# Batch 2's gate and value layer in seven products in place of eight, its weight sums made in batch 1, and the passage to layer two by halves in batches 2 and 3

## The chip, the cores and the metric

One core of one Trainium2 chip runs the whole program. The metric is the device time of one execution in microseconds (us), the median of several runs. A difference under about 0.3% (3.1 us here) can't be told from none.

## What is computed

Linear attention on 4 batches of 8 heads, 576 positions, then two feed-forward layers on the 2304 tokens, all in fp32:

```python
proj = q @ w_phi                      # and k @ w_phi; 64 -> 128 features
proj = proj - max(abs(proj), -1)      # phi = [exp(proj), exp(-proj)]
x = (phi_q @ (phi_k.T @ v)) / (phi_q @ sum(phi_k) + 1e-6)   # tokens x 512
x = leaky_relu(x @ w_in) @ w_out                            # layer one, d_ff 2048
g = x @ w_gate                                              # layer two, d_ff 1536
out = (g * sigmoid(g) * (x @ w_val)) @ w_out2
```

## The kernel before, in words

Work goes batch by batch. The activations of a batch lie with features on the 128 partitions and the 576 tokens (`S`) along the row; a product is made for half of the tokens at a time (`HT` = 288 columns), so that a result fits one PSUM bank. To reach fp32 accuracy every operand is split into a high and a low part of type fp32r: ScalarE copies the high part (`cp`, L90), VectorE subtracts it from the value for the low part (`sub`, L78). A product of two such operands is three matmuls: high by high, high by low, low by high.

A layer-one or gate or value tile of 128 output features takes 4 (the 512 inputs) x 3 = 12 matmuls a half, 24 a tile (`u_l1` L840, `u_gate` L848, `u_val` L859, all through `products` L811). An output block of layer one or two (`u_out` L873) takes four tiles' results at a time, 12 matmuls a half, and is added up in `acc` over the chunks of four.

Where a layer is done "in seven", two such tiles (rows 0 and 1 of weights) by two halves of tokens make a 2 x 2 block product, which `Quad` (L956) computes with seven block products instead of eight: `p1` to `p7`, six matmuls each (`six`, L929). For this it needs sums of the blocks of x (`x_sums_f32` L905) and of the weights (`mix` L788). `Quad` leaves partial results in PSUM bank `a` (p1, then p6, p5 and p3 on top) and bank `e` (p7, then p4 on top). ScalarE copies `a` out after p1, p6 and p5 (`u1`, `u2`, `u4`) before the next product may go on top of it, and VectorE adds them (`add` L990).

Before the change, batch 3 is in seven in both layers (`seven` L1091), batch 2 in layer one only (`seven_beside` L1154); batches 0, 1 and layer two of batch 2 are in eight. While batch b is in its two feed-forward layers, the attention of batch b + 1 runs beside it: its steps for k in layer one, those for q in layer two (`spread`, L1251), evenly over the list of units. A unit is one call of the list `units`; the weights of a unit are loaded and split when the unit four places before it is reached (`slots`, L1217). Each step is written down in the order of the program, and a scheduler then sets the order on each engine.

Weights: the fp64 inputs are turned into fp32 in batch 0 on ScalarE and VectorE (`f32_steps`), kept in HBM (`kept`), split in batch 1 (`w_split` L756), and from then on loaded as parts. The sums for `gX`, `gY`, `vX`, `vY` that batch 3's layer two needs were made beside batch 2's layer two (`w_sums` L797, called at L1292): two loads, four VectorE operations of 256 columns and two stores for each of 12 pairs of tiles. Buffers in SBUF: `wi` has 8 of 4 KB a partition for raw weights and split gate, value and layer-one tiles; `wo` has 5, `wr` 4.

```python
two(x.p1, x.p2, w=[("1", b, 4 * m)])                     # seven_beside, L1179
if not last or halves[-1] == 0:                          # u_out, L887: the parts of x2
    return                                               # are made once both halves are there
```

## Time and profile before

| | |
|---|---|
| median of 3 runs | 1045.04 us (1044.15 to 1047.02) |
| the profiled execution's own time | 1046.1 us |
| its span, first to last instruction | 1044.3 us |
| TensorE (PE) matmul busy | 1035.1 us, 99%, 7638 matmuls |
| weight loads (PEld) busy | 1017.0 us, 97% |
| VectorE (DVE) busy | 791.9 us, 76% |
| ScalarE (ACT) busy | 648.1 us, 62% |
| granted TensorE clock | 1.00 throughout |

Matmuls are pipelined, so the busy time of PE says little of how dense they are; the number of matmuls in a stretch against its length says more. The stages stand in the trace so: opening to 57 us; batch 0 to about 317; batch 1 to 574 (its layer two from about 437); batch 2's layer one to 690, its layer two from 704 to 834; batch 3's layer one to 933, its layer two to the end.

### The profile page before, as it was taken

How to read it: one execution, taken by the hardware profiler on the slowest of the kernel's cores; microseconds unless marked ns; L12 is line 12 of the kernel's file. 1: busy time of each engine (PE TensorE's matmuls, PEld its weight loads, DVE VectorE, ACT ScalarE, POOL GpSimd, SP SyncE). 2: the span in 40 equal slices, each digit the busy share in tenths (PEclk: the TensorE clock that was granted, in tenths of full speed). 3: DMA queues.
4: the chain of work that ended last, by engine and by line, in shares of the span. 5: the costliest groups of instructions: out<-in, count | busy, mean ns of one | idle time of the engine just before them, and what ended most of it. 6: DMA issues, size and time to landing. Idle time of an engine off the chain costs nothing.

```text
span 1044.3 us, 20425 instructions
## 1 busy us (share of the span) xinstructions
PE 1035.1 (99%) x7638; PEld 1017.0 (97%) x7638; DVE 791.9 (76%) x1726; ACT 648.1 (62%) x1448; POOL 21.7 (2%) x57
## 2 busy tenths in 40 slices
PE   9999999999999999999999999999999999999998
PEld 8889999999999999999999999999999999999998
DVE  5988989799999989678776867768788532468463
ACT  6879988699976887456542667735453244436531
POOL 1001100000000000000000000000000000000000
PEclk9999999999999999999999999999999999999999
DMA  8239878367757987856534487266988496559531
GB/s 261 98 145 326 288 272 300 116 221 225 257 198 272 392 320 254 327 195 217 175 130 154 164 308 236 72 245 250 324 287 283 151 321 239 168 186 314 187 112 56
DMA packets 101491, 236.19 MB, mean 226 GB/s; under 512 B 19856, under 2 KB 35984, under 8 KB 101392
## 3 DMA queue, kind: packets, MB, share of 16 engines
q1 hardware_dynamic: 95888, 219.74, 60.7%
q0 software_dynamic: 4032, 14.68, 3.7%
q8 instruction: 61, 1.00, 0.4%
q10 hardware_dynamic: 1472, 0.46, 0.2%
q14 instruction: 38, 0.31, 0.1%
HBM read 169.30 MB, written 65.54 MB: 225 GB/s over the span
## 4 chain that ended last, share of the span: by engine, by line
PE 90%; ACT 4%; DVE 3%; DMA 2%; issue 1%; SPq 0%; ACTq 0%
PE pm L816 61%; PE pa L945 9%; PE pm L945 6%; PE pa L459 5%; PE pa L248 2%; PE pa L207 2%; PE pa L260 2%; DMA xl<-in_vt_dram 1%; ACT wr L691 1%; ACT wi L694 1%; DMA wi<-in_w_dram 1%; PE pa L367 1%; PE pa L366 1%; PE pa L420 1%; DVE xl L78 1%
## 5 line engine op out<-in xcount | busy, mean ns | idle before, releaser
L816 PE MATMUL pm<-xh,wi 128*128 128x288 f32 x1664 | 349.8, 297 | 0.2 <-ACT es L844 0.2
L816 PE MATMUL pm<-gp,wo 128*128 128x288 f32 x2172 | 328.8, 297 | 0.4 <-DVE acc L886 0.2
L816 PEld LDWEIGHTS pm<-gp,wo 128*128 128x128 f32 x2172 | 301.1, 188 | 1.9 <-ACT acc L90 0.5
L816 PEld LDWEIGHTS pm<-xh,wi 128*128 128x128 f32 x1664 | 271.2, 188 | 1.5 <-ACT es L844 0.5
L816 PE MATMUL pm<-xl,wi 128*128 128x288 f32 x832 | 246.2, 297 | 0.0
L816 PEld LDWEIGHTS pm<-xl,wi 128*128 128x128 f32 x832 | 156.2, 188 | 0.6
L886 DVE TENSOR_TENSOR acc<-pm,acc 128x288 f32<-128x288 f32 x160 | 70.6, 451 | 47.8 <-PE pm L816 47.1
L78 DVE TENSOR_TENSOR gp<-es,gp 128x576 fp32r<-128x576 f32 x94 | 70.6, 752 | 26.2 <-ACT gp L90 25.8
L90 ACT ACTIVATE gp<-es 128x576 fp32r<-128x576 f32 x94 | 65.3, 697 | 31.8 <-DVE es L864 26.9
L78 DVE TENSOR_TENSOR wi<-wr,wi 128x512 fp32r<-128x512 f32 x96 | 64.5, 683 | 9.0 <-ACT wi L737 8.0
L737 ACT ACTIVATE wi<-wr 128x512 fp32r<-128x512 f32 x92 | 58.1, 650 | 13.6 <-PE pm L816 5.5
L945 PE MATMUL pm<-xh,wi 128*128 128x288 f32 x272 | 62.0, 296 | 0.1
L78 DVE TENSOR_TENSOR fl<-ff,fh 128x512 fp32r<-128x512 f32 (+1 forms) x72 | 51.2, 714 | 11.8 <-ACT fh L90 11.5
L691 ACT ACTIVATE wr<-wi 128x512 f32<-128x512 f32 x68 | 47.5, 699 | 10.5 <-DVE wi L78 4.2
L719 DVE TENSOR_TENSOR wr<-wr,wi 128x512 uint16<-128x512 uint16 x68 | 50.9, 755 | 0.6
L465 ACT ACTIVATE dn<-pa 64x288 f32<-64x288 f32 x64 | 26.0, 406 | 36.4 <-PE pa L459 35.5
L90 ACT ACTIVATE fh<-ff 128x512 fp32r<-128x512 f32 (+1 forms) x72 | 47.4, 663 | 0.7
L694 ACT ACTIVATE wi<-wi 128x512 int32<-128x512 uint32 x68 | 47.7, 702 | 0.0
L945 PEld LDWEIGHTS pm<-xh,wi 128*128 128x128 f32 x272 | 46.2, 188 | 0.6 <-ACT xh L90 0.3
L844 ACT ACTIVATE es<-pm 128x288 f32<-128x288 f32 x72 | 31.2, 439 | 23.7 <-PE pm L945 14.7
L90 ACT ACTIVATE acc<-pm 128x288 f32<-128x288 f32 x64 | 27.9, 447 | 27.0 <-PE pm L816 26.9
L864 DVE SCALAR_TENSOR_TENSOR es<-pm,es 128x288 f32<-128x288 f32 x72 | 32.1, 448 | 15.4 <-PE pm L816 15.1
(222 smaller groups left out, 2096.9 us busy)
## 6 DMA issues: line engine op xcount, KB each, us to landing
wo<-parts SPq DMA_DIRECT2D x77, 512.0 KB, 5.0
wi<-parts SPq DMA_DIRECT2D x68, 512.0 KB, 5.6
parts<-wi SPq DMA_DIRECT2D x56, 512.0 KB, 5.7
wi<-in_w_dram SPq DMA_DIRECT2D x44, 512.0 KB, 5.2
wr<-kept SPq DMA_DIRECT2D x64, 256.0 KB, 5.1
parts<-wo POOLq DMA_DIRECT2D x28, 512.0 KB, 5.5
kept<-wr SPq DMA_DIRECT2D x40, 256.0 KB, 4.4
wi<-in_wg_dram SPq DMA_DIRECT2D x12, 512.0 KB, 5.6
```

Of the source, the lines that this page charges most:

```text
L78: keep(dve.tensor_tensor(out=o, in0=a, in1=b, op=ALU.subtract))
L90: keep(act.activation(o, a, AF.Copy))
L459: keep(pe.matmul(ps, w, x, start=(i == 0), stop=(i == len(ops) - 1)))
L691: after_opening(act.activation(t[0], high.bitcast(F32), AF.Abs, scale=REBIAS))
L694: after_opening(act.activation(low, low.bitcast(U32), AF.Copy, scale=2.0**-29))
L719: keep(dve.tensor_tensor(out=t16, in0=t16, in1=e16, op=ALU.add))
L737: i = act.activation(t[:, 0], r, AF.Copy)
L816: m = pe.matmul(ps, w, x[:, c], start=(i == 0), stop=(i == n - 1))
L844: act.activation(o, i, AF.Prelu, alpha=0.01)
L864: dve.scalar_tensor_tensor(out=g[:, c], in0=ps, scalar=0.5, in1=g[:, c], op0=ALU.mult, op1=ALU.mult)
L886: dve.tensor_tensor(out=acc[o][:, t], in0=ps, in1=acc[o][:, t], op=ALU.add)
L945: m = pe.matmul(ps, a, b, start=start and n == 0, stop=stop and n == 5, skip_group_check=True)
```

## The change

- Layer two of batch 2 is done by a new `second_beside` with `Quad` for gate and value: seven products for each pair of tiles. The list of its units starts with the last output blocks of layer one, then come six pairs of gate and value tiles; a pair with no output blocks in the queue (the first two, the fourth and the sixth) is 7 units of 12 matmuls, one with them (third and fifth) 11 units.
- The sums of gate and value weights are made in batch 1, in `w_split`, from the fp32 tiles that are there for the split anyway, and stored. `w_sums` with its 24 loads is gone. In batch 2 the sums are loaded and split into two parts (24 tiles of 512 columns); in batch 3 they are loaded as before.
- Passage to layer two in batches 2 and 3: the output blocks come in the order `BY_HALF`, first halves first; the parts of x2 are made by halves (`x2_half`), and only the three quarters that the seven products read; the sums of x2 are made in place in `acc` (`x_sums_in_place`), first those for p7 and p5, then the others. The first pair of batch 3's layer two starts with p1, p2 of gate and value, then both p7, and then p6, p6, p5.
- Buffers: `wi` 8 becomes 5, with 3 new ones of the same size (`wx`) for every second raw weight of batch 0 and for sums of x2 in batch 2; `wr` 4 becomes 5; gate and value tiles of batch 2 take `wo`. Weights are loaded at most 5 ahead in batches 2 and 3 (`depth`), 8 before.

```diff
+BY_HALF = ((0, 0), (1, 0), (2, 0), (3, 0), (0, 1), (2, 1), (1, 1), (3, 1))
...
-        tag = ("wi", 8)
-        if key[0] in "23":
+        tag = ("wi", 5)
+        if key[0] in "gv" and key[1] == QA:
+            tag = ("wo", 5)
...
@@ w_split
+        if len(kind) == 2 and b == QA:
+            wtile[key] = t = T([P, 2, 512], F32R, "wi", 5)
+            to_wtile(t, r)
+            return
...
+        if f % 2 == 0:
+            wf["even", kind] = r
+            return
+        even = wf.pop(("even", kind))
+        mix(even, r)
+        for name, x in (("X", even), ("Y", r)):
...
+                kept[kind + name, f // 2] = d = dram.tile([P, 512], F32, name=f"sums_{uid[0]}")
+                nc.sync.dma_start(out=d, in_=x)
...
+    def x2_half(b, o, t):
+        c = slice(HT * t, HT * t + HT)
+        if o < 2:
+            if t:
+                return
+            if o == 0:
+                x2h[b, "low"], x2l[b, "low"] = T([P, S], F32R, "xh", 8), T([P, S], F32R, "xl", 8)
+            to, h, l = slice(HT * o, HT * o + HT), x2h[b, "low"], x2l[b, "low"]
+        else:
+            if t == 0:
+                x2h[b, o], x2l[b, o] = T([P, S], F32R, "xh", 8), T([P, S], F32R, "xl", 8)
+            to, h, l = c, x2h[b, o], x2l[b, o]
+        cp(h[:, to], acc[o][:, c])
+        sub(l[:, to], acc[o][:, c], h[:, to].bitcast(F32))
...
+    def x_sums_in_place(b):
+        one, two = slice(0, HT), slice(HT, S)
+        rows = [[whole_x.pop((b, kt)) for kt in (k, k + 2)] for k in range(2)]
+        for x in rows:
+            sub(x[0][:, one], x[0][:, two], x[0][:, one])
+            sub(x[0][:, two], x[1][:, two], x[0][:, two])
+        for k, x in enumerate(rows):
+            sums_to_parts(0, k, x[0], b == QA)
+        for x in rows:
+            sub(x[1][:, two], x[1][:, two], x[0][:, one])
+            sub(x[1][:, one], x[1][:, one], x[1][:, two])
+        for k, x in enumerate(rows):
+            sums_to_parts(1, k, x[1], b == QA and k == 0)
...
+    def second_beside(b):
...
+            if not queue:
+                two(*([lambda: x_sums_in_place(b)] if p == 0 else []), x.p1, x.p2, w=[("g", b, 2 * p)])
+                two(y.p1, y.p2, w=[("v", b, 2 * p)])
+                two(x.p7, y.p7, w=[(gy, b, p), (vy, b, p)])
+                two(x.p6, y.p6, w=[(gx, b, p), (vx, b, p)])
+                two(x.p5, y.p5)
+                two(x.p3, y.p3)
+                two(x.p4, y.p4, w=[("g", b, 2 * p + 1), ("v", b, 2 * p + 1)])
...
-        return 4 if any(k[1] == 1 for k in nxt) else 8
+        if any(k[1] == 1 for k in nxt):
+            return 4
+        return 8 if nxt and nxt[0][1] == 0 else 5
```

How the instructions stand, at three places. The first is VectorE at the passage from layer one to layer two of batch 2, from the last output blocks of layer one (`acc`) on; `fl`, `pk`, `mm`, `mrow`, `top` belong to the attention of batch 3. Before:

```order
L78 TENSOR_TENSOR xl_9623<-acc_8645,xh_9622 128x576
L397 CAST mm_78<-top_9744 18x32
L886 TENSOR_TENSOR acc_8678<-pm_9654,acc_8678 128x288
L78 TENSOR_TENSOR pk_10581<-raw_10529,pk_10581 64x576
L78 TENSOR_TENSOR mm_78<-top_9744,mm_78 18x32
L78 TENSOR_TENSOR xl_9669<-acc_8678,xh_9668 128x576
L406 TENSOR_TENSOR mrow_9592<-mm_78,cst_sb 128x288
L78 TENSOR_TENSOR fl_9679<-ff_9675,fh_9678 128x576
L78 TENSOR_TENSOR fl_9740<-ff_9736,fh_9739 128x576
```

With the change:

```order
L894 TENSOR_TENSOR acc_8768<-pm_9744,acc_8768 128x288
L396 TENSOR_REDUCE top_9891<-pa_9842 18x32
L80 TENSOR_TENSOR acc_8735<-acc_8735,acc_8616 128x288
L80 TENSOR_TENSOR wx_9774<-acc_8616,wx_9774 128x576
L80 TENSOR_TENSOR wi_9939<-wr_9768,wi_9939 128x512
L1042 TENSOR_TENSOR vraw_9798<-pm_9800,vraw_9798 128x288
L80 TENSOR_TENSOR acc_8684<-acc_8768,acc_8684 128x288
L399 CAST mm_78<-top_9891 18x32
L80 TENSOR_TENSOR xl_9678<-acc_8768,xh_9677 128x288
L80 TENSOR_TENSOR acc_8735<-acc_8735 128x288
L1042 TENSOR_TENSOR xg_9819<-pm_9821,xg_9819 128x288
L80 TENSOR_TENSOR fl_9835<-ff_9831,fh_9834 128x576
```

Before, the last add of layer one is followed by the last low part of x2 (L78 `xl<-acc`) and by attention, then by the gate's L857. Now sums of x2 (`acc<-acc`), a low part of a sum (`wx`), a split of a weight sum (`wi<-wr`) and the gate's and value's adds (L1042) stand between them.

The second is TensorE in the same layer. Before, the first gate tile follows the last output block with its 24 matmuls in two banks:

```order
L816 MATMUL pm_9654<-mrow_9326,wo_9231 128x288
L816 MATMUL pm_9654<-pk_9327,wo_9231 128x288
L816 MATMUL pm_9654<-mrow_9326,wo_9231 128x288
L816 MATMUL pm_9654<-gp_9464,wo_9231 128x288 x3
L816 MATMUL pm_9654<-gp_9500,wo_9231 128x288 x3
L816 MATMUL pm_9691<-xh_9533,wi_9288 128x288
L816 MATMUL pm_9691<-xl_9534,wi_9288 128x288
```

With the change, at the end of y.p2 and the start of the two p7:

```order
L994 MATMUL pm_9821<-xh_9677,wo_9493 128x288
L994 MATMUL pm_9821<-xl_9678,wo_9493 128x288
L994 MATMUL pm_9821<-xh_9677,wo_9493 128x288
L994 MATMUL pm_9846<-wx_9774,wi_9713 128x288 x3
L461 MATMUL pa_9979<-fh_9834,kvh_8523 128x288
L368 MATMUL pa_10002<-pk_9996,wst_h 128x288
L369 MATMUL pa_10002<-pk_9996,wst_l 128x288
L994 MATMUL pm_9853<-wx_9774,wi_9718 128x288 x3
L994 MATMUL pm_9846<-wx_9777,wi_9713 128x288
L994 MATMUL pm_9853<-wx_9777,wi_9718 128x288
```

The two p7 read the sums of x2 in `wx`, whose low parts VectorE makes after the last add above, 24 matmuls of p1 and p2 and two of attention after the last output block.

The third is VectorE at the passage of batch 3. Before, from the last add of layer one:

```order
L886 TENSOR_TENSOR acc_11904<-pm_12601,acc_11904 128x288
L78 TENSOR_TENSOR acc_11857<-acc_11904,acc_11857 128x288
L78 TENSOR_TENSOR xl_12616<-acc_11904,xh_12615 128x576
L78 TENSOR_TENSOR xl_12640<-acc_11750,xh_12639 128x576
L78 TENSOR_TENSOR acc_11904<-acc_11904,acc_11857 128x288
L78 TENSOR_TENSOR xl_12644<-acc_11813,xh_12643 128x576
L78 TENSOR_TENSOR acc_11904<-acc_11904 128x288
```

With the change:

```order
L894 TENSOR_TENSOR acc_12015<-pm_12718,acc_12015 128x288
L80 TENSOR_TENSOR acc_11970<-acc_12015,acc_11970 128x288
L1042 TENSOR_TENSOR rb_12792<-pm_12783,dn_12781 128x288
L80 TENSOR_TENSOR xl_12653<-acc_12015,xh_12652 128x288
L80 TENSOR_TENSOR acc_12015<-acc_12015,acc_11970 128x288
L80 TENSOR_TENSOR xl_12759<-acc_11970,xh_12758 128x576
L80 TENSOR_TENSOR acc_12015<-acc_12015 128x288
L80 TENSOR_TENSOR xl_12767<-acc_11926,xh_12766 128x576
```

Before, six low parts of 576 columns (`xl`) followed the last add, two of x2's own and four of sums. Now a low part of 288 columns (`xl_12653`) and three of sums follow it.

## Rows read from the trace of the kernel before

**Rows 1.** The page, busy time of each engine over the span.

```profile
PE 1035.1 (99%) x7638; PEld 1017.0 (97%) x7638; DVE 791.9 (76%) x1726; ACT 648.1 (62%) x1448; POOL 21.7 (2%) x57
```

**Rows 2.** Stretches: length; PE, PEld, DVE, ACT, POOL busy (count); clock; DMA; GB/s.

```profile
57.00:182.00 125.00, 123.63 (x917) 120.93 (x917) 112.36 (x234) 109.78 (x260) 10.74 (x23) 1.00 0.74 264
182.00:304.00 122.00, 121.46 (x860) 117.39 (x858) 112.35 (x242) 105.33 (x218) 4.25 (x8) 1.00 0.61 201
...
439.00:574.00 135.00, 135.00 (x1023) 135.00 (x1022) 98.48 (x218) 65.24 (x142) 0.00 (x0) 1.00 0.51 174
574.00:690.00 116.00, 115.32 (x878) 114.33 (x877) 82.54 (x169) 74.10 (x161) 0.00 (x0) 1.00 0.56 194
...
704.00:737.00 33.00, 33.00 (x251) 33.00 (x250) 29.33 (x73) 17.80 (x40) 0.00 (x0) 1.00 0.72 258
737.00:778.00 41.00, 41.00 (x312) 41.00 (x311) 30.24 (x79) 18.56 (x44) 0.00 (x0) 1.00 0.90 315
778.00:802.00 24.00, 24.00 (x183) 24.00 (x182) 21.09 (x55) 10.65 (x25) 0.00 (x0) 1.00 0.83 291
802.00:834.00 32.00, 32.00 (x244) 32.00 (x243) 21.14 (x46) 8.80 (x17) 0.00 (x0) 1.00 0.46 157
...
915.00:942.00 27.00, 26.14 (x191) 25.23 (x190) 18.15 (x39) 9.31 (x18) 0.00 (x0) 1.00 0.60 204
```

**Rows 3.** Chain of waits: start, us, piece (a run of 72 matmuls).

```profile
677.81 9.51 PE pm L816 x72
```

**Rows 4.** VectorE, timeline in batch 2's layer two: start, duration, instruction.

```profile
779.32 0.75 DVE L78 TENSOR_TENSOR gp<-es,gp 128x576 fp32r<-128x576 f32 x1
779.99 0.45 DVE L857 SCALAR_TENSOR_TENSOR es<-es,pm 128x288 f32<-128x288 f32 x1
780.36 0.45 DVE L78 TENSOR_TENSOR xl<-xf,xh 128x288 fp32r<-128x288 f32 x1
...
781.76 0.48 DVE L370 TRANSPOSE_TENSOR_REDUCE cst_sb<-pa 128x9 f32<-128x288 f32 x1
782.16 0.42 DVE L864 SCALAR_TENSOR_TENSOR es<-pm,es 128x288 f32<-128x288 f32 x1
782.51 0.74 DVE L78 TENSOR_TENSOR fl<-ff,fh 128x576 fp32r<-128x576 f32 x1
783.16 0.45 DVE L864 SCALAR_TENSOR_TENSOR es<-pm,es 128x288 f32<-128x288 f32 x1
```

**Rows 5.** VectorE groups in batch 1's layer two: busy, mean ns.

```profile
L78 DVE TENSOR_TENSOR wi<-wr,wi 128x512 fp32r<-128x512 f32 x17 | 11.7, 685 | 2.5 <-ACT wi L737 2.2
```

**Rows 6.** VectorE groups in batch 2's layer two (weight sums, gate and value).

```profile
L864 DVE SCALAR_TENSOR_TENSOR es<-pm,es 128x288 f32<-128x288 f32 x24 | 10.6, 446 | 4.4 <-PE pm L816 4.3
L857 DVE SCALAR_TENSOR_TENSOR es<-es,pm 128x288 f32<-128x288 f32 x24 | 10.6, 444 | 2.0 <-ACT es L856 1.8
L78 DVE TENSOR_TENSOR wr<-wr,wr 128x256 f32<-128x256 f32 x24 | 9.8, 407 | 0.1
...
L792 DVE TENSOR_TENSOR wr<-wr 128x256 f32<-128x256 f32 x12 | 5.1, 423 | 10.6 <-DMA wr<-kept 10.5
L78 DVE TENSOR_TENSOR wr<-wr 128x256 f32<-128x256 f32 x12 | 4.8, 403 | 0.1
```

**Rows 7.** TensorE, timeline at the passage of batch 3: start, duration, instruction.

```profile
934.01 0.29 PE L945 MATMUL pa<-xh,wi 128*128 128x288 f32 x1
934.38 0.40 PE L945 MATMUL pm<-xh,wi 128*128 128x288 f32 x1
934.95 0.40 PE L945 MATMUL pa<-xh,kvl 128*128 128x288 f32 x1 [0.17 <-ACT xh L90]
...
938.90 0.29 PE L945 MATMUL pa<-xh,kvl 128*128 128x288 f32 x1
939.31 0.40 PE L945 MATMUL pa<-xl,kvh 128*128 128x288 f32 x1
939.55 0.29 PE L945 MATMUL pa<-xh,kvh 128*128 128x288 f32 x1
940.34 0.40 PE L945 MATMUL pa<-xh,kvl 128*128 128x288 f32 x1 [0.50 <-ACT raw L90]
940.58 0.30 PE L945 MATMUL pa<-xl,kvl 128*128 128x288 f32 x1
```

**Rows 8.** The page, DMA issues: KB each, median us to landing.

```profile
wo<-parts SPq DMA_DIRECT2D x77, 512.0 KB, 5.0
...
wr<-kept SPq DMA_DIRECT2D x64, 256.0 KB, 5.1
```

More of the change, by code (lines that the diff above doesn't have):

```diff
@@ L886, in u_out @@
                 dve.tensor_tensor(out=acc[o][:, t], in0=ps, in1=acc[o][:, t], op=ALU.add)
-        if not last or halves[-1] == 0:
+        if not last:
+            return
+        if kind == "1" and b >= QA:
+            for t in halves:
+                x2_half(b, o, t)
+            if halves[-1]:
+                whole_x[b, o] = acc.pop(o)
+            return
+        if halves[-1] == 0:
             return
@@ L1051, in c22 @@
         def c22(self, u4):
+            if self.b == QA and self.kind != "1":
+                self.add(u4, self.e, u4)
+                self.finish(self.g[1][:, HT:S], u4)
+                return
             self.add((self.g[1] if self.kind == "1" else self.c)[:, HT:S], self.e, u4)
@@ L1063, in c21 @@
         def c21(self):
+            if self.b == QA and self.kind != "1":
+                self.add(self.u2, self.e, self.u2)
+                self.finish(self.g[1][:, 0:HT], self.u2)
+                if self.kind != "g":
+                    to_parts(self.g[1], ("3", self.b, 2 * self.p + 1))
+                return
             self.add((self.g[1] if self.kind == "1" else self.c)[:, 0:HT], self.e, self.u2)
@@ L1152, in seven, with o, two @@
                 unit(all_of(o(), o()))
+    def second_beside(b):
+        queue = [(h, o, t) for h in held for o, t in BY_HALF]
+        held.clear()
+        late = {}
+        def o():
+            (k, bb, c, last), oo, t = queue.pop(0)
+            fn = lambda: u_out(k, bb, c, oo, last, (t,))
+            if t == 0:
+                late[fn] = out_key(k, bb, c, oo)
+            return fn
+        def two(*fns, w=()):
+            return unit(lambda: [fn() for fn in fns], list(w) + [late[fn] for fn in fns if fn in late])
+        while queue:
+            two(o(), o())
+        for p in range(NF2 // 2):
+            x, y = Quad("g", p, 0, b), Quad("v", p, 1, b)
+            gx, gy, vx, vy = (kind + part for kind in "gv" for part in "XY")
+            if not queue:
[6 more added lines that the diff above has]
+                two(x.p4, y.p4, w=[("g", b, 2 * p + 1), ("v", b, 2 * p + 1)])
+            else:
+                two(x.p1, x.p2, w=[("g", b, 2 * p)])
+                two(x.p7, x.p6, w=[(gy, b, p), (gx, b, p)])
+                two(y.p1, y.p2, w=[("v", b, 2 * p)])
+                two(x.p5, y.p7, w=[(vy, b, p)])
+                two(x.p3, y.p6, w=[(vx, b, p)])
+                two(x.p4, o(), w=[("g", b, 2 * p + 1)])
+                two(y.p5, o())
+                two(o(), o())
+                two(o(), y.p3)
+                two(o(), o())
+                two(o(), y.p4, w=[("v", b, 2 * p + 1)])
+            if p % 2:
+                h = ("3", b, p // 2, p == NF2 // 2 - 1)
+                if h[-1]:
+                    held.append(h)
+                else:
+                    queue += [(h, o, t) for o in range(KD) for t in range(2)]
     def seven_beside(b):
```

112 lines of the change are left out of this document (58 added, 54 removed).

## The prediction, before the change was run

> **What bounds the kernel now.** I read the busy times first. TensorE's matmuls cover 99% of the span and its weight loads 97%, VectorE 76%, ScalarE 62% [rows 1]. Busy time says little of a pipelined engine, so I next took the pace of matmuls: in the chain of waits 72 of them, each 288 columns, take 9.51 us [rows 3], 132 ns each. Then the stretches [rows 2]. At that pace the 1023 matmuls of batch 1's layer two need 135.1 us and have 135.0; in batch 2's layer two the four pieces between 704 and 834 us hold 251, 312, 183 and 244, which need 33.1, 41.2, 24.2 and 32.2 us and have 33, 41, 24 and 32. So from about 300 us on TensorE sets the time, nothing waits, and a matmul less is 132 ns less. Two places differ. In batch 0, 860 matmuls need 113.5 us and take 122 (182 to 304), where VectorE and ScalarE are 92% and 86% busy. At batch 3's passage into layer two, 191 need 25.2 us and take 27.
>
> The clock is granted in full in every stretch, also where TensorE waits [rows 2], and I leave it there.
>
> The other limit to watch is VectorE where the change adds work. In the piece from 704 to 737 us it is busy 29.33 us of 33 [rows 2], and TensorE still loses nothing. A row's duration is not what it costs there: 576 columns last 0.75 us but the next instruction starts 0.67 us later (779.32, 779.99), 288 columns last 0.45 and cost 0.37 (779.99, 780.36), a reduction costs 0.40 (781.76, 782.16) [rows 4]. From the first two 512 columns cost about 0.60, an estimate, where they last 0.685 [rows 5].
>
> **The change, part by part**, against the profiled execution's 1046.1 us. It is 1.1 us above the median of 1045.04; I apply the sum to the median.
>
> 1. Matmuls. Batch 2's gate and value were 24 tiles of 24, 576 matmuls; six pairs of seven products of 2 x 6 leave 504. 72 go, each on the path: -9.5 us [rows 3].
>
> 2. VectorE in batch 2's layer two. What goes are the 48 operations of the weight sums there, 0.4 us each as rows last [rows 6], some 16 us by what they cost. What comes: three adds more a tile pair and kind, 36 x 0.37 = 13.3 us (next to the same 48 gate and value operations [rows 6]); 24 splits of weight sums x 0.60 = 14.4; eight sums of x2 and their four low parts, 5.6. So 33 come for 16, in a stage that gets 9.5 us shorter. Spread evenly that would fit: 101.8 us busy of 130 us in the four pieces [rows 2] becomes some 119 in 120. It isn't spread evenly. The units of the new layer are short (12 matmuls) where no output blocks are queued, attention steps are dealt out by units, and the first two pairs are of that kind. I counted the changed order from the first output half of the last chunk of layer one (the add on `acc`) to the last add of the second pair: 107 VectorE instructions. They are 8 output adds (3.0), 6 halves of x2 (2.2), 8 sums and 4 low parts of 576 (5.6), 8 weight splits (4.8), 25 gate and value operations and 2 low parts (10.6), and 46 of attention and of the next batch's sums: 7 of 576 columns (4.7), 3 on half the partitions (2.3), 7 reductions (2.8), 15 of about 288 columns (5.9), 14 small ones (2.1 by 0.15 each). Together 44.0 us. TensorE has 274 matmuls between the same two points, 36.3 us. The excess is 7.7. From there to the end of attention it is 122 instructions, by the same prices 50 us, against 434 matmuls, 57.4: VectorE catches up. TensorE can run ahead of it only a little, since the four PSUM banks of this layer are all in use (`a` and `e` of gate and value): I allow two products, 1.6 us. So about +6. Bounds: 0 if what is behind in the queue is not what TensorE waits for; +14 if the durations of rows 4 count in full (51.5 us against 36.3, less a slack of 1).
>
> The Trainium skill, "VectorE: DVE Perf Modes", section "Mode 1× (REGULAR) — the baseline", gives one result a cycle for such adds (0.96 GHz): 288 columns in 0.30 us. By it the 107 instructions would take about 35.5 us, an estimate from that page, the excess would be gone and the sum would be 6 us lower. The trace disagrees: 0.37 from start to start, with no wait between [rows 4]. That page's "Terms" name a flush of the pipe after every operation, which is of that kind.
>
> 3. The tight chain in the short units. In a pair without output blocks x.p5 comes six matmuls (0.8 us) after x.p6, and between them ScalarE must copy bank `a`. Where that stood so at batch 3's passage, TensorE's next matmul started 0.79 us after the last in place of 0.13 (939.55 to 940.34, released by that copy) [rows 7]. Two such places in each of the fourth and sixth pair (in the first two VectorE is the later one): 4 x 0.35 = +1.4. Bounds 0 and 8 x 0.66 = +5.3.
>
> 4. Passage of batch 3. In rows 7 the starts lie 0.37, 0.57, 0.24 (934), 0.41, 0.24, 0.79 and 0.24 us (939 to 940) apart in place of 0.13: 1.9 us lost. In the new order both parts of x2's needed quarters are made before the last add, 24 matmuls of p1 and p2 (3.2 us) stand before the first p7, and after the last add VectorE has to do 2.5 us before that p7 is served (six instructions of 288 columns or less, one of 576, at the prices above, of which not all are before it). I take -1.5; bounds 0 and -1.9.
>
> 5. Passage of batch 2. Before, nothing is lost there (251 in 33.0 us) [rows 2]; its new sums are inside part 2. No gain.
>
> 6. Batch 1. The 48 sum operations move there, 16 us at cost, with 24 stores. VectorE goes from 98.5 to some 114 us of 135, 85%, ScalarE stays at 65 [rows 2]. Batch 1 hides that; if its cover is short, gate and value adds are late next. I take 0, bounds 0 and +3.
>
> 7. Buffers. In batch 0 `wi` and `wx` share what `wi` had, `wr` has one more, and the order of all engines is another; TensorE loses some 12 us there now (3.5 to 182 us, 8.5 to 304) [rows 2]. I take 0, bounds -2 and +2. In batches 2 and 3 a `wi` buffer is freed at the closest 48 matmuls (6.4 us) before it is needed again, where it was 103 (13.7 us), counted in the two orders; a transfer lands in 5.0 to 5.1 us [rows 8]. Still hidden, 0 by itself.
>
> Sum: -9.5 + 6.0 + 1.4 - 1.5 = -3.6, so 1041.4 us (own time 1042.5).
>
> **The rivals.** *VectorE keeps up* (0.12). The lag of part 2 falls on attention, whose results aren't needed for 100 us. For it: 89% busy without a lost matmul [rows 2]. Against: VectorE works in order, and gate and value adds stand behind that attention. Then -9.5 - 1.5 and 0 to 1.4: 1034 to 1036.
>
> *VectorE takes it all* (0.36). The excess is paid in full, 7.7, and the short units lose the 7% that batch 0 loses where VectorE and ScalarE are both near 90% [rows 2], on the 60 us after: another 2 to 5. Then 1042 to 1048, no difference that can be told.
>
> *Late weights* (0.19), the other side. SyncE's queue issues in order. A load of a weight sum into `wr` waits for a buffer that a second-of-pair tile holds until p4; the `wi` and `wo` loads behind it wait too, with 6.4 us in hand and 5.1 needed. From a wait of 1.3 us on, TensorE waits for the weight. At 8 such loads in batch 2's two layers and 1 to 2 us each that is 8 to 16 us on the forecast: 1048 to 1057. For it: eight buffers became five, and depth 8 became 5. Against: weights of eight and seven both landed in time in batch 2 before, with margins of 13 us.
>
> **How the numbers follow.** The forecast's own case is 0.33, at 1036 to 1042. With the first rival, faster by over 0.3% (below 1041.9; 0.3% is about what can be told from no change) has 0.45; within 0.3% 0.36; slower 0.19. Range: from 1034.5, where VectorE keeps up, to 1050, which leaves out the worse half of late weights.
>
> **What would show it.** Right: 7566 matmuls in place of 7638; at batch 3's passage no start gap above 0.3 us; in batch 2's layer two a stretch of about 40 us from the passage on where VectorE is busy without a gap and TensorE has 6 us fewer matmuls than it could hold; then full pace. Wrong: full pace through that stretch (first rival), waits on weight loads by DMA (third), or gaps before L994's matmuls in every pair down to the sixth (second). A batch 0 that is longer or shorter by over 2 us would make the forecast wrong without touching its argument.

## The result, and the profile after

The changed kernel takes 1057.85 us (median of 4 runs, 1056.52 to 1061.93), the kernel before beside it 1045.12: a ratio of 1.0126, 95% interval 1.0095 to 1.0158. Slower, where 1041.4 was forecast. The profiled execution took 1061.93 us, against 1046.1 before: it is the slowest of the four, 4.1 us above their median, so a loss read from it below can be up to that much larger than in the median one.

The page's busy times, against [rows 1]:

```profile
PE 1037.4 (98%) x7566; PEld 1013.9 (96%) x7566; DVE 823.1 (78%) x1802; ACT 672.8 (63%) x1516; POOL 22.1 (2%) x57
```

The 72 matmuls are gone and TensorE is busy longer. The stretches against [rows 2]: length; PE, PEld, DVE, ACT, POOL busy (count); clock; DMA; GB/s:

```profile
57.00:182.00 125.00, 122.21 (x895) 119.49 (x894) 110.49 (x228) 107.61 (x255) 11.13 (x23) 0.99 0.73 261
182.00:304.00 122.00, 120.59 (x854) 116.21 (x853) 110.13 (x233) 101.52 (x210) 4.25 (x8) 1.00 0.62 202
439.00:574.00 135.00, 135.00 (x1022) 135.00 (x1021) 113.31 (x266) 68.12 (x153) 0.00 (x0) 1.00 0.67 234
...
704.00:720.00 16.00, 13.40 (x93) 12.13 (x91) 15.81 (x41) 8.42 (x19) 0.00 (x0) 1.00 0.60 198
720.00:736.00 16.00, 14.17 (x100) 13.05 (x98) 15.14 (x37) 13.58 (x32) 0.00 (x0) 1.00 0.41 141
736.00:752.00 16.00, 15.39 (x103) 15.15 (x104) 14.45 (x35) 9.89 (x23) 0.00 (x0) 0.89 0.53 178
752.00:768.00 16.00, 12.65 (x73) 12.05 (x72) 10.37 (x26) 7.85 (x19) 0.00 (x0) 0.79 0.42 142
...
800.00:816.00 16.00, 14.35 (x105) 13.83 (x105) 15.45 (x37) 11.23 (x26) 0.00 (x0) 1.00 0.81 285
```

A piece of 16 us at full pace shows 123 matmuls in this view (before, 720 to 736 us; the line stands further down); the pieces from 704 us show 93, 100, 103, 73 and (at 800) 105. The clock column, 1.00 throughout before, falls to 0.89 and 0.79 there. Batch 1's layer two runs at full pace with VectorE at 113.31 us, as the prediction had it.

The two executions do the same matmuls in the same order up to batch 2's layer two, so starts of the same matmul can be compared. Batch 0 is 4.4 us longer (matmul 2400 starts at 349.5 us, before at 345.1), batch 1 nothing, batch 2's layer one 0.3 (matmul 5000: 693.2 against 688.5). From there to the matmul that is 1450 from the end it is 168.8 us, before 157.1. Before, these were 1187 matmuls at full pace; now they are 1115, which would take 147.6. So 21.2 us are lost there, and 9.5 gained. Batch 3 is as long as before. 4.4 + 0.3 + 21.2 - 9.5 is 16.4; the last matmul starts 16.3 us later.

Where TensorE waits longest in batch 2's layer two (its timeline: start, duration, instruction, idle time before it and what ended it):

```profile
755.38 1.06 PE L994 MATMUL pm<-wx,wi 128*128 128x288 f32 x6 [0.56 <-DVE xg L1042]
759.23 0.61 PE L994 MATMUL pm<-xh,wi 128*128 128x288 f32 x1 [2.78 <-ACT vraw L92]
759.63 0.44 PE L994 MATMUL pm<-xl,wi 128*128 128x288 f32 x1
759.87 0.68 PE L994 MATMUL pm<-xh,wi 128*128 128x288 f32 x2
```

It waits for ScalarE's copy of a PSUM bank (`vraw`). ScalarE at that time:

```profile
753.59 0.44 ACT L1098 ACTIVATE es<-vraw 128x288 f32<-128x288 f32 x1
757.67 0.63 ACT L744 ACTIVATE wi<-wr 128x512 fp32r<-128x512 f32 x1 [3.64 <-DMA wr<-sums]
758.21 0.67 ACT L92 ACTIVATE gp<-es 128x576 fp32r<-128x576 f32 x1
758.78 0.39 ACT L92 ACTIVATE vraw<-pm 128x288 f32<-128x288 f32 x1
```

It stood 3.64 us before the split of a weight sum whose transfer had not landed, and the copy that TensorE needed stood two places behind. In the layer (690 to 825 us) this wait of ScalarE adds up to (us in total, times, longest):

```profile
ACT wi L744 <- DMA wr<-sums: 11.2, 5, 3.6
```

TensorE's other waits of 1 us or more in the layer were for VectorE (2.6, 1.5, 1.2 and 1.0 us in total), and none was for a transfer: so the wait at 759.23 is the longest, not the only kind.

And why the transfer was late, from SyncE's queue:

```profile
744.94 5.97 SPq L660 DMA_DIRECT2D wo<-parts  x4
751.00 1.30 SPq L660 DMA_DIRECT2D wr<-parts  x1
752.36 1.54 SPq L685 DMA_DIRECT2D wr<-sums  x3
754.00 0.38 SPq L660 DMA_DIRECT2D wo<-parts  x1
759.05 0.32 SPq L685 DMA_DIRECT2D wr<-sums  x1
```

Three of the pair's four sums are asked for together at 752.36, behind tiles that wait for their buffers, and the fourth after the first has been split (759.05). ScalarE's wait ends at 757.67, some 5 us after the first was asked for. A pair puts six tiles through the five `wr` buffers: four raw sums and two second tiles, which stay until p4. That the number of these buffers is what makes the sums late is a reading of this queue; the run after_wr4 does not bear it out.

The passage of batch 3, against [rows 7]:

```profile
955.69 0.40 PE L994 MATMUL pa<-xl,kvh 128*128 128x288 f32 x1 [0.34 <-DVE xl L80]
...
956.72 0.40 PE L994 MATMUL pa<-xh,kvl 128*128 128x288 f32 x1 [0.24 <-ACT raw L92]
...
958.29 0.40 PE L994 MATMUL pa<-xh,kvh 128*128 128x288 f32 x1 [0.50 <-ACT kvz L92]
```

The waits are later in the order, not gone: the first is now p6's, for the low part of a sum of x2. From the 800th to the 700th matmul from the end it is 15.2 us, before 15.2.

### The profile page after: what moved, and what is told of

Its sections match the earlier page's. It is cut to its first block, busy times and chain, and to the rows that moved or that the text cites. A ratio compares the mean times of both kernels' runs of the same rounds, so it can differ in the third digit from the quotient of the medians.

```text
span 1060.2 us, 20479 instructions
## 1 busy us (share of the span) xinstructions
PE 1037.4 (98%) x7566; PEld 1013.9 (96%) x7566; DVE 823.1 (78%) x1802; ACT 672.8 (63%) x1516; POOL 22.1 (2%) x57
## 4 chain that ended last, share of the span: by engine, by line
PE 76%; DVE 9%; ACT 8%; DMA 4%; issue 2%; SPq 0%; POOL 0%; ACTq 0%; DVEq 0%; POOLq 0%
PE pm L821 46%; PE pa L994 9%; PE pm L994 8%; PE pa L461 4%; DMA wr<-sums 2%; PE pa L250 2%; PE pa L262 2%; DMA wi<-in_w_dram 1%; PE pa L209 1%; ACT wr L698 1%; PE pm L520 1%; DVE wi L80 1%; DVE fl L80 1%; ACT gp L92 1%; PE pm L365 1%
## 5 line engine op out<-in xcount | busy, mean ns | idle before, releaser
L821 PE MATMUL pm<-gp,wo 128*128 128x288 f32 x2100 | 322.2, 298 | 5.0 <-ACT acc L92 2.1
L821 PEld LDWEIGHTS pm<-gp,wo 128*128 128x128 f32 x2100 | 293.0, 189 | 8.2 <-ACT acc L92 2.5
L821 PE MATMUL pm<-xh,wi 128*128 128x288 f32 x1280 | 270.4, 298 | 0.2 <-ACT es L852 0.2
L821 PEld LDWEIGHTS pm<-xh,wi 128*128 128x128 f32 x1280 | 208.5, 188 | 1.5 <-ACT es L852 0.5
L821 PEld LDWEIGHTS pm<-xl,wi 128*128 128x128 f32 x640 | 120.0, 188 | 0.7
L894 DVE TENSOR_TENSOR acc<-pm,acc 128x288 f32<-128x288 f32 x160 | 70.6, 451 | 39.7 <-PE pm L821 38.7
L744 ACT ACTIVATE wi<-wr 128x512 fp32r<-128x512 f32 x116 | 73.7, 650 | 39.9 <-DMA wr<-sums 12.0
L80 DVE TENSOR_TENSOR wi<-wr,wi 128x512 fp32r<-128x512 f32 x120 | 81.0, 682 | 14.6 <-ACT wi L744 13.5
L994 PE MATMUL pm<-xh,wi 128*128 128x288 f32 x344 | 81.2, 299 | 2.8 <-ACT vraw L92 2.8
L994 PEld LDWEIGHTS pm<-xh,wi 128*128 128x128 f32 x344 | 60.0, 191 | 3.5 <-ACT vraw L92 3.0
L994 PE MATMUL pm<-xl,wi 128*128 128x288 f32 x172 | 51.4, 299 | 0.0
L220 ACT ACTIVATE ff<-pa,mn 128x128 f32<-128x128 f32 x80 | 33.8, 434 | 8.9 <-DVE mn L218 8.4
L994 PE MATMUL pa<-xh,kvh 128*128 128x288 f32 x160 | 37.8, 295 | 0.5 <-ACT kvz L92 0.5
L994 PE MATMUL pa<-xh,wi 128*128 128x288 f32 x160 | 37.8, 295 | 0.0
```

Source lines behind the costliest of these rows:

```text
L80: keep(dve.tensor_tensor(out=o, in0=a, in1=b, op=ALU.subtract))
L220: act.activation(f[:, h, 0], pv[:, h], AF.Exp, bias=mn[:, h : h + 1])
L744: i = act.activation(t[:, 0], r, AF.Copy)
L821: m = pe.matmul(ps, w, x[:, c], start=(i == 0), stop=(i == n - 1))
L894: dve.tensor_tensor(out=acc[o][:, t], in0=ps, in1=acc[o][:, t], op=ALU.add)
L994: m = pe.matmul(ps, a, b, start=start and n == 0, stop=stop and n == 5, skip_group_check=True)
```

## The experiments

Each row is a kernel with its start of matmul 5000 (all that happens ahead of batch 2's layer two), what it loses in that layer (measured as above, against 147.6 us; for eight products against 157.1), its median, and its ratio to the kernel before. The first two columns come from the profiled execution. A helper's line has another number in some of these kernels (`Quad`'s products are L989, L991, L994 or L995).

| kernel | matmul 5000 | lost | median us | ratio (95%) |
|---|---|---|---|---|
| before | 688.5 | 0.0 | 1045.12 | |
| the change | 693.2 | 21.2 | 1057.85 | 1.0126 (1.0095 to 1.0158) |
| eight_b2 | 693.1 | 0.0 | 1050.26 | 1.0040 (1.0025 to 1.0055) |
| sums_parts | 704.4 | 7.4 | 1056.90 | 1.0111 (1.0095 to 1.0128) |
| att_hole | 693.7 | 24.1 | 1060.57 | 1.0154 (1.0130 to 1.0177) |
| split_pool | 692.7 | 19.5 | 1061.90 | 1.0164 (1.0147 to 1.0181) |
| sums_wx | 694.8 | 7.4 | 1049.68 | 1.0041 (1.0026 to 1.0056) |
| sums_wx_wr4 | 690.6 | 7.4 | 1045.62 | 1.0000 (0.9989 to 1.0011) |
| sums_wx_late | 692.9 | 7.5 | 1048.98 | 1.0035 (1.0025 to 1.0045) |
| sums_wx_raw | 693.1 | 7.3 | 1048.27 | one run |
| wr4_att11 | 690.4 | 5.4 | 1043.72 | 0.9988 (0.9977 to 1.0000) |
| wr4_att18 | 690.3 | 12.3 | 1050.44 | 1.0045 (1.0028 to 1.0063) |
| wr4_raw | 694.9 | 7.4 | 1050.28 | 1.0046 (1.0031 to 1.0060) |
| wr4_idle_split | 694.2 | 7.3 | 1048.40 | 1.0024 (1.0011 to 1.0037) |
| wr4_split_placed | 690.1 | 12.8 | 1050.97 | 1.0054 (1.0040 to 1.0068) |
| after_wr4 | 690.9 | 16.9 | 1054.30 | 1.0082 (1.0067 to 1.0098) |
| wr4_pace8 | 690.3 | 4.1 | 1041.37 | 0.9964 (0.9951 to 0.9976) |
| wr4_pace11 | 690.3 | 6.6 | 1044.72 | 0.9993 (0.9984 to 1.0002) |
| after_wr4_pace8 | 690.2 | 18.1 | 1054.63 | 1.0081 (1.0061 to 1.0101) |
| wr4_pace8_early | 690.3 | 3.3 | 1041.40 | 0.9958 (0.9943 to 0.9972) |

My theory after the result was **late weights**: the splits wait for late transfers and ScalarE, which works in order, holds PSUM copies behind them. The rival was **VectorE overload**, the prediction's own term.

**eight_b2**: what is the seven products', and what the rest of the change's. (Its other edits put back the tiles, loads and parts of x2 that only the seven products need in batch 2.)

```diff
...
-        if b == QA:
-            second_beside(b)
-        else:
-            flush()
-        for f in range(NF2 if b != QA else 0):
+        flush()
+        for f in range(NF2):
```

> Batch 2's layer two is back in eight products; buffers, weight sums made in batch 1 and the passage of batch 3 stay as in the change. In the trace of the change TensorE is 4.4 us later than before when batch 1 begins, loses some 21 us in batch 2's layer two and is not faster at batch 3's passage. All theories: the 72 matmuls come back (+9.5), the 21 us of stalls go, so about 1049 us (1047 to 1051), 4 us over the kernel before, and those 4 us lie in batch 0. If it comes out at 1045 or below, batch 0's loss was chance of that run; if above 1053, the moved weight sums or the smaller buffers cost more than the trace showed.

1050.26, as expected. Without the seven products nothing is lost in batch 2's layer two; 4.6 us are lost ahead of it, nearly all in batch 0.

**sums_parts**: the sums split in batch 1, where their fp32 values are at hand, and loaded as parts.

```diff
-            if kind == "1":
-                t = T([P, 2, 512], F32R, "wi", 5)
-                to_wtile(t, x)
-                unkept.append(((kind + name, f // 2), t))
-            else:
-                uid[0] += 1
-                kept[kind + name, f // 2] = d = dram.tile([P, 512], F32, name=f"sums_{uid[0]}")
-                nc.sync.dma_start(out=d, in_=x)
+            t = T([P, 2, 512], F32R, "wi", 5)
+            to_wtile(t, x)
+            unkept.append(((kind + name, f // 2), t))
```

> The weight sums of gate and value are split in batch 1 and loaded as parts in batch 2, so that no split of a weight sum stands in ScalarE's and VectorE's queues there and wr holds no raw sums. Theory late weights (the split waits for a late transfer and ScalarE, which works in order, holds the PSUM copies behind it): 10 to 14 us come back, 1044 to 1048 us. Theory VectorE overload (too many VectorE operations in the first two pairs): the 8 splits there are 5 us of it, 1052 to 1054 us. Both allow 0 to 3 us more in batch 1, where VectorE then is busy some 128 of 135 us.

By the total both theories missed. By stages, 13.8 us come back in batch 2's layer two (some 4 us less if the change's loss is taken at its median), and 11 are lost ahead of it. In batch 1 (480 to 500 us, waits by engine) ScalarE's splits wait for the sums that VectorE makes and for a `wi` buffer that is being stored, and TensorE for a split; that the `wi` buffers are the cause of the 11 us is shown by sums_wx below.

```profile
PE pm L816 <- ACT wi L744: 1.5, 1, 1.5
...
ACT wi L744 <- DVE wr L80: 3.1, 2, 2.1
ACT wi L744 <- DMA parts<-wi: 1.7, 1, 1.7
```

**att_hole**: attention kept out of the first two pairs.

```diff
-        places = list(range(lo, hi))
+        places = [i for i in range(lo, hi) if not i in hole]
...
+    hole = range(bounds[QA][1] + 4, bounds[QA][1] + 18)
...
+        if b == QA:
+            mid -= 10
```

> Batch 3's attention stays out of the first two pairs of batch 2's layer two: its q steps start ten units earlier, in layer one, and leave out the 14 units of these pairs. Theory VectorE overload: the first two pairs lose nothing any more, 6 to 9 us come back, 1049 to 1052 us. Theory late weights: the loads of the sums are as late as before, 0 to 2 us come back, 1056 to 1058 us.

Slower, 24.1 us lost; neither theory had that. It told little of VectorE's load: the attention that starts earlier was still being worked off at the passage (25 of its matmuls from 704 to 718 us, 11 in the change), and ScalarE still waited 7.7 us for the sums (stretches, columns as above):

```profile
704.00:718.00 14.00, 14.00 (x108) 13.96 (x106) 13.66 (x33) 9.12 (x19) 0.00 (x0) 1.00 0.59 192
718.00:732.00 14.00, 10.14 (x47) 8.60 (x46) 13.26 (x31) 7.95 (x20) 0.00 (x0) 0.76 0.26 93
```

**split_pool**: GpSimd splits the sums in batch 2.

```diff
-            to_wtile(t, r)
+            pool.tensor_copy(out=t[:, 0], in_=r)
+            pool.tensor_tensor(out=t[:, 1], in0=r, in1=t[:, 0].bitcast(F32), op=ALU.subtract)
             return
```

> In batch 2 GpSimd splits the weight sums, both parts, in place of ScalarE and VectorE; buffers and loads stay. Theory late weights, in-order ScalarE: a late sum now stops only GpSimd, TensorE waits for the weight itself at most: 8 to 14 us come back, 1044 to 1050 us, unless GpSimd takes over 3 us for a split. Theory VectorE overload: the 8 splits of the first two pairs go, 5 us come back, 1052 to 1054 us. Theory of the tight chain through the PSUM banks in short units: no change in pairs four and six.

Both missed. GpSimd needs 0.76 us for the copy and 1.48 for the subtraction, so 2.2 for a split, less than the 3 us that late weights allowed; it still waits for the sums, and it slows VectorE, which is told in the last section. The run decides nothing between the two.

**sums_wx, sums_wx_wr4, sums_wx_late, sums_wx_raw.** The first mends sums_parts: in batch 1 the split sums of gate and value go through `wx`. The others change one thing more: all `"wr", 5` to 4; `mid + (12 if b == QA else 0)` for the start of the q steps; `raws[0] % 3 == 1` for `raws[0] % 2`.

```diff
-            t = T([P, 2, 512], F32R, "wi", 5)
+            t = T([P, 2, 512], F32R, *(("wx", 3) if kind in "gv" else ("wi", 5)))
```

> As sums_parts, but in batch 1 the split sums of gate and value go through the three wx buffers, which are idle there, and not through the five wi. In sums_parts TensorE was 7.5 us later in batch 1's layer two and 3.4 us in batch 2's layer one, while ScalarE's splits waited for wi tiles that were still being stored. Theory buffers: those 11 us go, batch 2's layer two keeps the 14 us that sums_parts won there: 1044 to 1048 us. Theory VectorE overload in batch 1 (128 of 135 us busy): 3 us or less come back, 1053 to 1057 us.

> sums_wx with four wr buffers, as before the change, in place of five. No raw sums stand in wr any more, so batch 2 should not feel it. If the fifth buffer is why batch 0 became 4.4 us longer (conversions are taken up earlier and stand in ScalarE's queue ahead of PSUM copies), batch 0 is 3 to 4 us shorter than in sums_wx; if the split into wi and wx is the reason, no change (within 1 us).

> sums_wx with the q steps of batch 3's attention starting twelve units later, in the second pair of batch 2's layer two. Theory VectorE overload, for what is still lost there (7.6 us in sums_parts, of which 6 lie between 715 and 735 us of its trace): 3 to 5 us faster than sums_wx. If the loss comes from the chain between TensorE, ScalarE and VectorE through the PSUM banks alone, no change; if the denser attention overloads the pairs after it, 0 to 3 us slower.

> sums_wx with two of three raw weights of batch 0 in wx in place of one of two, which balances the use of wi and wx there. If batch 0 is longer because wi is short (its raw and its split tiles share five buffers), batch 0 becomes 2 to 4 us shorter; if the fifth wr buffer is the reason, no change.

sums_wx keeps the 13.8 us and loses 1.6 ahead of the layer in place of 11, with VectorE at 124.48 of 135 us in batch 1: so `wi`'s buffers were the cause there, though the total is 1.7 us above the range. The first 16 us of batch 2's layer two are no better without the raw sums. In sums_wx_wr4 they are

```profile
704.00:720.00 16.00, 14.13 (x93) 12.26 (x92) 15.81 (x39) 11.23 (x26) 0.00 (x0) 1.00 0.74 284
```

with the 93 matmuls and the 15.81 us of VectorE of the change: late sums are not needed to explain what the change loses there.

The fifth `wr` buffer costs 4.2 us up to matmul 5000, 3.1 of them in batch 0 (matmul 2400 at 349.8 and 346.7). Of these, 1.7 are a stretch at half clock that not every execution has: sums_wx_late, whose edit leaves batch 0 alone, comes to matmul 2400 at 348.0 without it (last section). The buffer lets conversions of raw weights be taken up sooner, and they stand on ScalarE ahead of PSUM copies. ScalarE in the change, batch 0:

```profile
92.08 0.97 ACT L698 ACTIVATE wr<-wi 128x512 f32<-128x512 f32 x1
92.65 0.96 ACT L701 ACTIVATE wi<-wi 128x512 int32<-128x512 uint32 x1
93.22 0.90 ACT L744 ACTIVATE wi<-wr 128x512 fp32r<-128x512 f32 x1
93.74 0.94 ACT L698 ACTIVATE wr<-wx 128x512 f32<-128x512 f32 x1
94.29 0.95 ACT L701 ACTIVATE wx<-wx 128x512 int32<-128x512 uint32 x1
94.85 1.59 ACT L92 ACTIVATE acc<-pm 128x288 f32<-128x288 f32 x4
```

and TensorE's next matmul:

```profile
95.59 2.63 PE L821 MATMUL pm<-gp,wo 128*128 128x288 f32 x11 [2.12 <-ACT acc L92]
```

In the 200 matmuls from the 400th on ScalarE does 10 such conversions in the change (70.6 to 101.2 us), 8 with four buffers (70.6 to 98.2).

sums_wx_late tested nothing: the first attention matmuls stood at 700 us as before, since the scheduler takes up what is ready. sums_wx_raw was 1.6 us quicker in batch 0, about the 1.7 us of half clock that it did not have; the same edit with four buffers (wr4_raw) was 1.7 slower there, and its total lies outside both of its expectations: no telling.

**wr4_att11, wr4_att18, wr4_raw, wr4_idle_split**, all from sums_wx_wr4. To hold the attention back, its first matmul is put in the order of the units; the steps start 11 or 18 units into layer two. wr4_raw has the edit of sums_wx_raw, and wr4_idle_split adds 24 splits of a constant.

```diff
-            keep(pe.matmul(ps, wst_h, a, start=True, stop=False))
+            m = pe.matmul(ps, wst_h, a, start=True, stop=False)
+            if b == QB:
+                tc.stamp_issue_order_token(m.ins, "units")
...
-        spread(q_steps(b + 1), mid, end - 3)
+        spread(q_steps(b + 1), mid + (11 if b == QA else 0), end - 3)
```

> sums_wx_wr4, in which the 7.6 us still lost in batch 2's layer two lie between 700 and 735 us of its trace (VectorE busy 34.9 of 36 us) and at 795. sums_wx_late did not test VectorE's load: the scheduler had taken the attention up as early as before. Here batch 3's first attention matmul of each q step is held in the order of the units, and the steps start with the second pair. Theory VectorE overload: the first pair's loss falls, 3 to 5 us faster than sums_wx_wr4 (1041 to 1043 us). Theory chain through the PSUM banks: the loss stays, 1045 to 1046 us.

> As wr4_att11, the steps starting with the third pair. Theory VectorE overload: both first pairs run at full pace, but VectorE then has about 89 of 94 us to do behind them: between 1040 and 1046 us, with the losses moved to the third to sixth pair. Theory chain: the loss at 700 to 735 us stays.

> sums_wx_wr4 with two of three raw weights of batch 0 in wx. Batch 0 of sums_wx_wr4 still ends 1.6 us later than before the change. If its wi buffers are short, 1 to 2 us come back (1043.5 to 1044.5 us); if it is the order of the engines, no telling, within 1 us.

> sums_wx_wr4 with the 24 splits of weight sums put back into ScalarE's and VectorE's queues in batch 2 at their places, but of a constant that is always there, into a scratch tile: the work of the splits without the wait for a transfer. Theory late weights: 0 to 3 us more than sums_wx_wr4, 1045 to 1049 us. Theory that the time of the splits is what cost 14 us: most of the 14 us come back, 1055 us or more.

wr4_att11 loses 2.0 us less in the layer, less of a gain than VectorE overload had; in wr4_att18 the loss moves (7 us between 780 and 800) and grows to 12.3, beyond what was expected. So the place of attention does cost or give back some us. wr4_idle_split was misplaced: its 24 idle splits were taken up between 570 and 636 us.

**wr4_split_placed, after_wr4, wr4_pace8, wr4_pace11.** The first puts the idle splits where they were meant to be; the last two keep the hold of wr4_att11 and deal out attention by matmuls in place of by units, from 8 or 11 units into layer two on. after_wr4 is the change with four `wr` buffers.

```diff
+        def idle_split(self, o):
+            t = T([P, 256, 2], F32, "dm", 1)
+            x = o.rearrange("p (f o) -> p f o", o=1).to_broadcast([P, 256, 2])
+            act.activation(t, x, AF.Copy)
+            sub(t, x, t)
...
+    long = [12] * 5 + [18, 18, 24, 18, 24, 18]
+    cost = [24] * 4 + [12] * 14 + long + [12] * 7 + long + [12] * 7
+    def spread_by_matmuls(steps, lo, hi, start):
+        total = sum(cost[start:])
+        for k, todo in enumerate(steps):
+            i = start
+            while sum(cost[start:i + 1]) <= total * k / len(steps):
+                i += 1
+            atts.setdefault(lo + i, []).append(todo)
...
+            spread_by_matmuls(q_steps(b + 1), mid, end, 8)
...
```

> In wr4_idle_split the scheduler took up the 24 idle splits in batch 2's layer one (570 to 636 us), so it told nothing of layer two. Here each reads a result of its own pair of tiles (four in each pair, of 512 columns, into a scratch tile), so that they stand between that pair's operations on ScalarE and VectorE, and none waits for a transfer. Theory late weights: sums_wx_wr4 plus 0 to 4 us, 1045 to 1050 us, the loss between the passage and the last matmul of batch 2's layer two at most 12 us. Theory that the time of the splits costs the 14 us: 1055 us or more, the loss near 21 us.

> The changed kernel with four wr buffers in place of five and nothing else. Batch 0 and 1: 3 us come back, as between sums_wx and sums_wx_wr4, if the fifth buffer is the cause. Batch 2's layer two: theory late weights says that a raw sum then waits for its buffer longer still, so the loss there grows from 21 us to 25 to 35 and the time is 1058 to 1070 us; theory VectorE overload says that it stays at 21 us, 1054 to 1056 us.

> sums_wx_wr4 with batch 3's q steps held in the order of the units as in wr4_att11, but dealt out by matmuls instead of by units, from the fifth unit of the first pair to the end of layer two. Theory VectorE overload: less is lost than in wr4_att11 (1043.7 us), 1041 to 1043.5 us, since VectorE's work is then even over TensorE's. Theory chain: what is left at the passage and in the short pairs does not depend on attention, 1043.5 to 1045 us.

> As wr4_pace8, the steps starting with the second pair. Theory VectorE overload: 1041 to 1043.5 us; if the steps that end later hold batch 3's layer one up, slower than wr4_att11.

The splits' time without the wait for transfers costs 5.4 us (7.4 to 12.8). It is not quite the splits' time alone, since ScalarE waits 9.7 us in front of the idle splits for the results of VectorE that they read. The total is 1 us beyond what late weights allowed and 4 short of the other theory. With the raw sums and the same four buffers (after_wr4) 16.9 are lost: of the 9.5 us between this and 7.4, more than half is the splits' time, and 4.1 (2.5 by the medians, less what lies ahead of the layer) is waiting for transfers, half clock included.

after_wr4 went against late weights: with a buffer less ScalarE waits about as long as in the change, and not more is lost.

```profile
ACT wi L744 <- DMA wr<-sums: 11.7, 5, 4.0
```

Of the 4.3 us that it loses less, 3.1 are the profiled executions (the change's lies 4.1 us above its median, this one's 1.0), so 1.2 us are left. Its total is where VectorE overload had it. Its batch 0 fits the buffer's 3 us (matmul 2400 at 346.7). wr4_pace8 is 0.4% faster than the kernel before; wr4_pace11 is not, and is slower than expected.

**after_wr4_pace8, wr4_pace8_early.** after_wr4_pace8 and wr4_pace8 have the same buffers and the same attention, and the sums raw or as parts. wr4_pace8_early asks for the first pair's sums with the last output blocks of layer one.

```diff
+        first = [(kind + part, b, 0) for part in "YX" for kind in "gv"]
         while queue:
-            two(o(), o())
+            two(o(), o(), w=[first.pop(0)])
...
-                two(x.p7, y.p7, w=[(gy, b, p), (vy, b, p)])
-                two(x.p6, y.p6, w=[(gx, b, p), (vx, b, p)])
+                two(x.p7, y.p7, w=[(gy, b, p), (vy, b, p)] if p else [])
+                two(x.p6, y.p6, w=[(gx, b, p), (vx, b, p)] if p else [])
...
```

> after_wr4 (1054.3 us, 16.9 us lost in batch 2's layer two) with the pacing of attention of wr4_pace8 and nothing else: the raw sums are still loaded and split in batch 2. Theory VectorE overload: with attention spread over TensorE's work the splits find room, 7 us or more come back, 1045 to 1048 us. Theory late weights: the splits still wait for transfers with the PSUM copies behind them, 0 to 4 us come back, 1050 to 1054 us.

> wr4_pace8 (1041.4 us), where TensorE waits 1.7 us at 709.7 us for the first pair's weight sum, whose load stands behind loads of output weights in SyncE's queue. Here the first pair's four sums are asked for with the last output blocks of layer one. If that wait is the transfer's alone, 1 to 2 us come back, 1039.5 to 1040.5 us; if the sums of x2 or the PSUM copies are late next, under 0.7 us.

With attention spread out and the raw sums kept, nothing comes back: 18.1 us lost, and the total is 0.6 us above late weights' range. The same stretches as above in after_wr4_pace8, and the wait in the layer:

```profile
704.00:720.00 16.00, 12.72 (x84) 11.09 (x83) 10.87 (x24) 7.53 (x17) 0.00 (x0) 1.00 0.37 132
720.00:736.00 16.00, 13.56 (x87) 12.62 (x86) 12.96 (x30) 9.74 (x22) 0.00 (x0) 0.91 0.52 165
736.00:752.00 16.00, 15.34 (x113) 14.97 (x112) 14.54 (x36) 10.32 (x26) 0.00 (x0) 0.98 0.71 252
752.00:768.00 16.00, 15.20 (x101) 14.88 (x102) 12.63 (x29) 10.54 (x25) 0.00 (x0) 0.89 0.53 175
```

```profile
ACT wi L746 <- DMA wr<-sums: 14.2, 8, 3.2
```

VectorE is no longer full in the first piece (10.87 of 16 us) and TensorE has 84 matmuls where 123 fit: here it is the transfers that hold it (in the chain that ended last, followed back from 720 to 704 us, the sums' transfers have the largest share, 38%). The same in wr4_pace8_early, where ScalarE has no such wait:

```profile
704.00:720.00 16.00, 15.11 (x107) 13.98 (x106) 12.86 (x32) 7.46 (x17) 0.00 (x0) 1.00 0.61 195
720.00:736.00 16.00, 16.00 (x122) 16.00 (x122) 14.33 (x33) 11.65 (x29) 0.00 (x0) 1.00 0.75 279
736.00:752.00 16.00, 16.00 (x122) 15.94 (x121) 14.07 (x37) 10.05 (x24) 0.00 (x0) 1.00 0.56 211
752.00:768.00 16.00, 16.00 (x124) 16.00 (x122) 11.61 (x27) 9.30 (x23) 0.00 (x0) 1.00 0.68 254
```

The earlier request gains 0.8 us in the layer and nothing in the median; the 1.7 us wait for the weight gave way to starts that are 0.35 to 0.4 us late, four times, in the first pair. This kernel and wr4_pace8 are faster than the change by 16 us and than the kernel before by 0.4%.

## Why the prediction was wrong

*Matmuls (-9.5): right.* 7566 of them, and when everything else is taken away (wr4_pace8_early) all but 3.3 us of the 9.5 are there.

*Buffers (part 7): the step that failed.* "Still hidden, 0 by itself" was counted on `wi`, 6.4 us against a transfer of 5.0 to 5.1 [rows 8]. The raw sums go through `wr`, for which no count was made there; and the engine that waits for them is ScalarE, 11.2 us in the layer, with the copies of PSUM behind. Raw sums against parts, with the same buffers and the same attention, is 16.9 against 7.4 with attention as in the change, 9.5 us, and 18.1 against 4.1 with attention spread out, 14.0 us (13.3 by the medians). Of the 9.5, 4.1 are waiting and 5.4 the splits' time by these executions; how the 14.0 divide no run shows. Which buffer or queue makes the sums late stays open.

The rival *late weights* had the queue, the buffer held until p4 and a price of 8 to 16 us (1049 to 1057 by its own sum, not 1048), but let TensorE wait for the weight itself, which it does nowhere in the layer, and was given 0.19. That 1057.85 lies just beyond its end is in part luck: the 4.7 us ahead of the layer and what VectorE costs beyond the forecast are in the measured time and not in its price.

*Batch 0 (part 7): mis-sized.* 0 with bounds of -2 and +2; it is +4.4, of which the fifth `wr` buffer is 3, and 1.7 of these the clock. A buffer more was taken for a help or nothing, where ScalarE is 86% busy and the scheduler takes up what is ready.

*VectorE (part 2): right in kind, mis-sized.* +6 was forecast, and 1.4 for part 3. Without the raw sums but with their splits' time 12.8 us are lost, without either 7.4, and 4.1 when attention is dealt out by matmuls: so 5.4 us hang on the splits' time and 3.3 on the places of attention. ScalarE's half of the splits (20 conversions of 0.62 us each in the layer) had no term. The throughput sum (44.0 us for 36.3) asked only for the excess; that a nearly full engine is also late for each result on which the next product depends is my reading, and no run tests it by itself. The busy share alone does not tell: before, VectorE was busy 15.60 of 16 us from 720 to 736, and TensorE lost nothing.

```profile
720.00:736.00 16.00, 16.00 (x123) 16.00 (x123) 15.60 (x44) 7.31 (x16) 0.00 (x0) 1.00 0.91 326
```

By the rate in the Trainium skill ("VectorE: DVE Perf Modes", section "Mode 1× (REGULAR) — the baseline"), one result a cycle, the forecast would have been 6 us lower (0.30 us for 288 columns, an estimate from that page). The measured cost, 0.37 [rows 4], was the better guide, and the result lay on the other side of the forecast.

So of the 16.4 us by which the forecast was too low, 4.7 lie ahead of the layer, 1.5 in batch 3's passage and 5.4 in VectorE's term (12.8 less 6.0 and 1.4); that leaves some 5 for waiting. It is a rough sum, as its parts come from profiled executions.

*The tight chain (part 3, +1.4): too large.* In wr4_pace8_early no start gap from 715 us to the end of the layer is above 0.30 us (0.13 at full pace), the fourth and sixth pair included.

*Passage of batch 3 (part 4, -1.5): 0.* All was staked on the first p7. The sums for p7 were there in time; p6, 12 matmuls later, needs the sums that VectorE makes last, and the chain from p6 to p5 through ScalarE is as it was.

*Batch 1 (part 6, 0): right.* *The clock: missed.* "I leave it there" held for the kernel before, whose longest wait behind the opening is 0.7 us; a forecast with waits has to price their clock too.

Open are why a `wr` buffer less does not make the layer lose more, and what the 1.8 us are that the best kernel still loses ahead of it.

## What to carry to other kernels

When a change loads something new, count for each buffer it goes through how many tiles a period puts there and which of them stays longest, and ask which engine's in-order queue will stand before the late one, and what stands behind it. Do the conversion where the data is already at hand and hidden, and load the finished form: 24 splits moved a stage earlier were worth 9.5 us here with attention as it was and 14 with attention spread out. Work that a scheduler fills in beside the critical engine is to be dealt out by that engine's time, not by counting steps, and held by a dependency; a later place in the program alone moved nothing.
